# Attention and gated layer on one core: the first head in pieces, probabilities added in pairs on GpSimd, nine key blocks from head 10

## The chip, the cores and the metric

The kernel runs on 1 core of a Trainium2 chip. The metric is the device time of one execution in microseconds; three runs of the kernel before took 936.40, 937.06 and 937.13 us. The engines are named as in the profile: PE is TensorE (matmuls), PEld its weight loads, DVE is VectorE, ACT is ScalarE, POOL is GpSimd, SP is SyncE, which issues DMAs.

## The reference

Attention over q and k of 4 batches × 8 heads × 1152 positions × 64, the query positions averaged in twos, and then a gated layer on the concatenated heads:

```python
q_pool = q.reshape(B, H, S // 2, 2, D).mean(axis=3)
scores = scale * np.matmul(q_pool, k.transpose(0, 1, 3, 2))
scores = scores - np.max(scores, axis=-1, keepdims=True)
attn = np.exp(scores); attn = attn / (np.sum(attn, -1, keepdims=True) + 1e-09)
x = (attn @ v).transpose(0, 2, 1, 3).reshape(B * S // 2, H * D)
out = (1 / (1 + np.exp(-(x @ w_gate))) * (x @ w_val)) @ w_out
```

So there are 32 heads of 576 queries and 1152 keys, and a layer 512 -> 1536 -> 512 over 2304 rows.

## The kernel before, in words

Heads are taken one after the other, in pairs (0 and 1, 2 and 3, ...), eight to a batch. Each head has two halves of 288 queries (`GR`), and each half nine blocks of 128 keys. For a block, two matmuls make the scores in a PSUM bank (line 472: the operands are split in a high and a low part, and the second matmul also carries the maximum of each query, subtracted by a diagonal matrix). ACT makes the exponential (line 476, tile `eh`), in heads 8 and later a second time in full precision (line 504), DVE makes the difference `el` (line 507), and PE multiplies both with V (lines 514 and 518). In heads 0 to 7 (`WHOLE`) one matmul in full float32 does it (line 489, tiles `e` and `ve`).

The sums of the probabilities, from head 8 on, come in two ways. Of the blocks in `POOLC(u)` (seven of nine in heads 8 to 13, nine of nine from head 14) POOL adds the `eh` tiles one by one into `acc` (line 536). A block outside it costs one more matmul, of `eh` with ones (line 521). At the end of a half ACT makes the high part of `acc` (line 576, tile `dh`), DVE the low part (line 579), and two matmuls with ones (line 583) put the sum into the bank of the low products.

Before a head's scores its operands are made (`head_operands`): q and K are loaded by SP (lines 303 and 300), POOL adds the two query positions (line 316), ACT makes the high parts (lines 321 and 336), DVE or POOL the low parts (lines 326 and 342). Then the maxima: twelve matmuls of 128 queries × 384 keys (line 375), each reduced by DVE (line 380), and the four query tiles' maxima joined (line 390) and written as diagonals into the low operand (line 358, on DVE for head 0, on POOL after it). The last 64 queries of the two heads of a pair share three more matmuls: SP copies their operands together (lines 404 and 405, `KP` and `QP`), and POOL writes their diagonals (line 413).

The gated layer of a batch (`gated`, line 699 for its matmuls, line 756 its low parts on POOL) is interleaved with the heads of the next batch, and the last batch's layer stands alone at the end. The weights are converted during heads 0 to 7 and read back from memory.

The order on each engine is written out by a planner (`Plan`): every operation has an engine, an estimated duration, a priority, the operations it comes after and the buffers it takes (`SLOTS` says how many of each there are). The planner plays the work through with these durations and takes on each engine the ready operation of the lowest priority number; the sequence that comes out is the order on the engine's queue. On the chip each queue runs in that order, and an operation waits where it stands. PE's eight PSUM banks (`b`), eight `eh`, four `el`, two `acc` and two `dh` are the buffers that the halves share.

Of the kernel before, what the change touches and what calls it, by code (L numbers as in the profile page):

```python
# [9 lines left out]
F32 = mybir.dt.float32  # L10
# [12 lines left out]
class Op:  # L23
    def __init__(self, eng, dur, fn, prio, after=(), take=None, late=0.0, keep=0.0):
# [3 lines left out]
        self.users, self.start, self.end = [], None, None  # L28
# [9 lines left out]
class Plan:  # L38
# [16 lines left out]
    def op(self, eng, dur, fn, prio, after=(), uses=(), take=(), late=0.0, keep=0.0):  # L55
        o = Op(eng, dur, fn, prio, after, list(take), late, keep)
        for h in uses:
            o.after.append(h.ops[0])
        for h in list(take) + list(uses):
            h.ops.append(o)  # L60
        self.ops.append(o)
        return o

    def run(self):
        n_dep = {}
        ready = {e: [] for e in self.LAT}
        for k, o in enumerate(self.ops):
# [3 lines left out]
            for a in o.after:  # L71
                a.users.append(o)
        free = {t: [(0.0, s) for s in range(n)] for t, n in self.slots.items()}
# [24 lines left out]
        while done < len(self.ops):  # L98
# [7 lines left out]
            while again:  # L106
                again = False
                for e in self.LAT:
# [40 lines left out]
                    for u in o.users:  # L149
                        n_dep[u] -= 1  # L150
                        u.at = max(u.at, o.end if u.eng == e and e != "SP" else av)
# [7 lines left out]
def attention_glu_kernel(ctx: ExitStack, tc: tile.TileContext, qT, kT, vt_in, v, wg, wv, wo, out):  # L159
# [43 lines left out]
    def change_first():  # L203
# [10 lines left out]
    rc = const.tile([128, GN // 32], F32, name="rc")  # L214
    SK_T = lambda n: [const.tile([128, SK], F32R, name=f"{n}{i}") for i in range(SLOTS["K"])]
    SQ_T = lambda n: [const.tile([128, SQ + 64], F32R, name=f"{n}{i}") for i in range(SLOTS["Q"])]
    SHAPE = {"x": [128, 2, SQ], "wg": [128, 2, 2, 4, 128], "el": [128, GN], "acc": [128, GN],
# [12 lines left out]
        "eh": tiles("eh", [128, GN], F32R),  # L230
# [6 lines left out]
        "pm": tiles("pm", [128, 4, 4], F32),  # L237
# [49 lines left out]
    DGP = lambda u: u >= 1  # L287
    RUNS = (2, 5, 8)
    POOLC = lambda u: range(7 if u < 14 else NC)
    LO, HI = slice(0, 64), slice(64, 128)  # L290


    def head_operands(u, need):
        whole = WHOLE(u)
# [56 lines left out]
        am = maxima(need - 21, pm, 4, lambda t: tl(qh)[0][:, t * 128:(t + 1) * 128], lambda: tl(kh)[0],  # L351
                    lambda: tl(pm), max_in, [qh, kh])

        def diag(eng):
            nm = tl(pm)[:, :, 3]
            q2 = tl(qh)[1][LO, 0:512].rearrange("p (a c) -> p a c", c=64)
            for par, p in enumerate((LO, HI)):
                eng.tensor_tensor(  # L358
                    out=q2[:, par:8:2], in0=ident[p, p].unsqueeze(1).to_broadcast([64, 4, 64]),
                    in1=nm[p].unsqueeze(2).to_broadcast([64, 4, 64]), op=ALU.mult)  # L360

        if DGP(u):
            dg = pl.op("POOL", 1.5, lambda: diag(nc.gpsimd), need - 6, after=[am], uses=[pm, qh])
        else:
            dg = pl.op("DVE", 1.3, lambda: diag(nc.vector), need - 6, after=[am], uses=[pm, qh])
        return dict(k=kh, q=qh, v=vr, lv=lv, got=[dg] + max_in + rest, hi_k=hi_k, hi_q=hi_q)

    def maxima(at, pm, nt, lhs, rhs, out, after, uses):
        red = []
        for t in range(nt):  # L370
            for j in range(3):
                m = pl.hold("b")

                def mm(t=t, j=j, m=m):
                    nc.tensor.matmul(out=tl(m)[:, 0:384], lhsT=lhs(t), rhs=rhs()[:, j * 384:(j + 1) * 384],  # L375
                                     start=True, stop=True)

                def rmax(t=t, j=j, m=m):
                    o = out()[:, t, j:j + 1] if nt > 1 else out()[:, j:j + 1]
                    nc.vector.tensor_reduce(out=o, in_=tl(m)[:, 0:384], axis=AXX, op=ALU.max)  # L380
# [6 lines left out]
        def all_max():  # L387
            o = out()
            if nt > 1:
                nc.vector.tensor_reduce(out=o[:, :, 3], in_=o[:, :, 0:3], axis=AXX, op=ALU.max, negate=True)  # L390
            else:
                nc.vector.tensor_reduce(out=o[:, 3:4], in_=o[:, 0:3], axis=AXX, op=ALU.max, negate=True)  # L392
# [486 lines left out]
```

## Time and profile before

| | |
|---|---|
| median of three runs | 937.06 us |
| the profiled execution | 936.75 us |
| its span, first to last instruction | 935.0 us |
| PE busy | 910.1 us (97%) |
| DVE busy | 679.3 us (73%) |
| ACT busy | 658.5 us (70%) |
| POOL busy | 645.6 us (69%) |

The predicted time is that of a run; the rows come from the profiled execution, which is 1.75 us longer than its span. Heads 0 to 7 occupy about 16 to 153 us, heads 8 to 31 the time up to about 810 us (27 us each), and the last batch's gated layer the rest. PE's records overlap, since a matmul is recorded longer than the distance to the next; a duration per matmul is therefore taken from the distance of starts or from the chain.

### The profile page before, as it was taken

The page shows a single profiled execution, that of the slowest core. Times are in us where ns is not written, and L with a number is a line of the kernel's source. Part 1 is how long each engine was busy: PE and PEld are TensorE (multiplying, and loading weights), DVE is VectorE, ACT ScalarE, POOL GpSimd, SP SyncE. Part 2 cuts the span into 40 slices and gives each one's busy share as a digit, 9 for nine tenths or more (in the row PEclk, how much of TensorE's full clock was granted, in tenths as well). Part 3 has the DMA queues.
Part 4 walks back from the last instruction along what each step waited for, and adds up shares of the span by engine and source line. Part 5 has one row for each costly group of instructions (what it writes and reads, how often), then busy time and mean ns, then how long its engine had stood idle before and what let it go on. Part 6 is the DMA issues. An engine that isn't in the chain of part 4 may idle for free.

```text
span 935.0 us, 18634 instructions
## 1 busy us (share of the span) xinstructions
PE 910.1 (97%) x6312; PEld 878.3 (94%) x6312; DVE 679.3 (73%) x1466; ACT 658.5 (70%) x1701; POOL 645.6 (69%) x744
## 2 busy tenths in 40 slices
PE   5999999999999999999999999999999999999998
PEld 4887887999999999999999999999999999999998
DVE  6578678898899898888777988878778885510112
ACT  4888788989998777677877688677778767422211
POOL 6645456788788688788879889888878877521211
PEclk9999999999999999999999999999999999999999
DMA  8898988787868556554445545644554433444432
GB/s 182 211 283 250 263 260 250 240 262 227 277 200 281 169 206 190 149 161 112 144 126 148 175 132 152 179 147 132 154 152 130 142 113 113 158 142 161 178 113 74
DMA packets 57566, 166.87 MB, mean 178 GB/s; under 512 B 17536, under 2 KB 21632, under 8 KB 51328
## 3 DMA queue, kind: packets, MB, share of 16 engines
q1 hardware_dynamic: 57472, 165.70, 58.3%
q8 instruction: 49, 0.80, 0.4%
q14 instruction: 45, 0.37, 0.1%
HBM read 132.12 MB, written 23.59 MB: 167 GB/s over the span
## 4 chain that ended last, share of the span: by engine, by line
PE 86%; DVE 8%; ACT 4%; issue 1%; DMA 1%; POOL 0%; SPq 0%; ACTq 0%; POOLq 0%; DVEq 0%
PE bank L699 45%; PE bank L472 15%; PE bank L375 7%; PE bank L489 7%; PE bank L518 6%; PE bank L514 5%; DVE pm L380 2%; DVE dh L579 2%; PE bank L583 1%; DVE el L507 1%; DVE pp L380 1%; DMA kr<-in_kT_dram 1%; ACT e L476 1%; ACT eh L476 1%; POOL acc L536 0%
## 5 line engine op out<-in xcount | busy, mean ns | idle before, releaser
L699 PE MATMUL bank<-x,wg 128*128 128x288 f32 x2304 | 357.1, 295 | 2.1 <-DVE pp L392 1.2
L699 PEld LDWEIGHTS bank<-x,wg 128*128 128x128 f32 x2304 | 327.3, 188 | 3.8 <-DVE pp L392 1.4
L536 POOL TENSOR_TENSOR acc<-acc,eh 128x288 f32<-128x288 f32 x312 | 258.4, 828 | 52.6 <-ACT eh L476 37.2
L380 DVE TENSOR_REDUCE pm<-bank 128x1 f32<-128x384 f32 x384 | 204.8, 551 | 58.5 <-PE bank L375 54.3
L476 ACT ACTIVATE eh<-bank 128x288 fp32r<-128x288 f32 x432 | 176.7, 409 | 80.0 <-PE bank L472 72.0
L507 DVE TENSOR_TENSOR el<-bank,eh 128x288 fp32r<-128x288 f32 x432 | 192.9, 452 | 54.1 <-ACT bank L504 49.8
L472 PE MATMUL bank<-QA,KA 128*128 128x288 f32 x576 | 177.7, 311 | 2.6 <-ACT e L476 1.3
L504 ACT ACTIVATE bank<-bank 128x288 f32<-128x288 f32 x432 | 176.6, 409 | 0.1
L472 PE MATMUL bank<-QB,KB 128*128 128x288 f32 x576 | 169.2, 297 | 3.0 <-DVE QB L358 3.0
L756 POOL TENSOR_TENSOR g<-sg,g 128x288 fp32r<-128x288 f32 x96 | 79.1, 824 | 107.8 <-ACT g L752 105.8
L375 PE MATMUL bank<-KA,QA 128*128 128x384 f32 x384 | 131.9, 357 | 9.3 <-ACT KA L336 8.3
L699 PE MATMUL bank<-g,wo 128*128 128x288 f32 x864 | 139.1, 296 | 0.0
L514 PE MATMUL bank<-eh,vt 128*128 128x288 f32 x432 | 127.7, 296 | 0.9 <-DVE el L507 0.9
L518 PE MATMUL bank<-el,vt 128*128 128x288 f32 x432 | 127.9, 297 | 0.7 <-DVE el L507 0.7
L699 PEld LDWEIGHTS bank<-g,wo 128*128 128x128 f32 x864 | 125.7, 189 | 0.3 <-DVE pm L380 0.2
L472 PEld LDWEIGHTS bank<-QA,KA 128*128 128x128 f32 x576 | 109.3, 190 | 9.7 <-ACT e L476 2.9
L472 PEld LDWEIGHTS bank<-QB,KB 128*128 128x128 f32 x576 | 109.3, 190 | 4.9 <-issue 3.4
L748 DVE SCALAR_TENSOR_TENSOR sg<-sg,bank 128x288 f32<-128x288 f32 x96 | 43.2, 450 | 79.8 <-PE bank L699 77.9
L375 PEld LDWEIGHTS bank<-KA,QA 128*128 128x128 f32 x384 | 74.1, 194 | 13.4 <-ACT KA L336 8.6
L518 PEld LDWEIGHTS bank<-el,vt 128*128 128x128 f32 x432 | 81.3, 188 | 1.8 <-DVE el L507 1.5
L514 PEld LDWEIGHTS bank<-eh,vt 128*128 128x128 f32 x432 | 81.2, 188 | 1.5 <-DVE el L507 1.2
L742 ACT ACTIVATE sg<-bank 128x288 f32<-128x288 f32 x96 | 39.3, 409 | 56.7 <-PE bank L699 56.1
(67 smaller groups left out, 1254.6 us busy)
## 6 DMA issues: line engine op xcount, KB each, us to landing
wg<-wg_d SPq DMA_DIRECT2D x48, 1024.0 KB, 5.1
kr<-in_kT_dram SPq DMA_DIRECT2D x64, 288.0 KB, 5.3
wo<-wo_d SPq DMA_DIRECT2D x36, 512.0 KB, 3.9
wg_d<-cs SPq DMA_DIRECT2D x24, 512.0 KB, 4.8
qr<-in_qT_dram SPq DMA_DIRECT2D x32, 288.0 KB, 3.9
KP<-KA SPq DMA_DIRECT2D x32, 288.0 KB, 3.5
vr<-in_v_dram SPq DMA_DIRECT2D x24, 288.0 KB, 3.3
cr<-in_wg_dram SPq DMA_DIRECT2D x12, 512.0 KB, 5.7
```

Of the source, the lines that this page charges most:

```text
L375: nc.tensor.matmul(out=tl(m)[:, 0:384], lhsT=lhs(t), rhs=rhs()[:, j * 384:(j + 1) * 384], start=True, stop=True)
L380: nc.vector.tensor_reduce(out=o, in_=tl(m)[:, 0:384], axis=AXX, op=ALU.max)
L472: nc.tensor.matmul(out=tl(m)[:, 0:GN], lhsT=tl(hd["k"])[k][:, ks], rhs=tl(hd["q"])[k][:, a:b], start=(k == 0), stop=(k == 1))
L476: nc.scalar.activation(out=tl(eh), in_=tl(m)[:, 0:GN], func=ACTF.Exp, scale=1.0 / 16.0)
L489: nc.tensor.matmul(out=tl(av[0])[:, 0:GN], lhsT=pair(c, 0), rhs=tl(h), start=(c == 0), stop=(c == NC - 1))
L504: nc.scalar.activation(out=p, in_=p, func=ACTF.Exp, scale=1.0 / 16.0)
L507: nc.vector.tensor_tensor(out=tl(el), in0=tl(m)[:, 0:GN], in1=tl(eh).bitcast(F32), op=ALU.subtract)
L514: nc.tensor.matmul(out=tl(av[0])[:, 0:GN], lhsT=pair(c, w), rhs=tl(eh), start=(c == 0), stop=(c == NC - 1))
L518: nc.tensor.matmul(out=tl(av[1])[:, 0:GN], lhsT=pair(c, 1 - w), rhs=tl(el), start=(c == 0), stop=(c == NC - 1 and not mine_c))
L536: nc.gpsimd.tensor_tensor(out=tl(acc), in0=tl(e0).bitcast(F32) if two else tl(acc), in1=tl(e1).bitcast(F32), op=ALU.add)
L699: nc.tensor.matmul(out=ps[:, 0:GN], lhsT=l, rhs=r, start=(n == 0 and j == 0), stop=(n == 3 and j == 2))
L756: nc.gpsimd.tensor_tensor(out=g[:, 1, a:b], in0=tl(sg), in1=g[:, 0, a:b].bitcast(F32), op=ALU.subtract)
```

## The change

It has three parts and what goes with them.

Head 0 has its own operand code (`first_head`). q is loaded in two pieces of 384 and 192 columns by SP, K in two halves of 576 columns, the first issued from ACT's queue and the second from SP's; V follows. The sum of the two query positions is made on DVE, per piece, and so are the low parts of q. The 64 queries of the last tile are a fifth tile of the head itself, so there are fifteen maxima; the first nine (three query tiles, enough for the first half of 288) have their own joining and diagonals, on DVE, and the other six the same later, needed by the second half alone. Head 1 also gets five tiles and no shared tail. Three set-up operations are changed: a small Exp activation is put ahead of everything on ACT, and two of the three memsets of the K tiles go from DVE to POOL.

```diff
+    def first_head():
+        QS, KS, TS = ((0, 384), (384, SQ)), ((0, SQ), (SQ, SK)), ((0, 1, 2), (3, 4))
+                nc.sync.dma_start(out=tl(qr)[:, :, a:b], in_=qT[0][:, :, a:b])
+                def load_k(a=a, b=b, p=p, eng=nc.sync if k else nc.scalar):
+                    eng.dma_start(out=tl(kr)[p, a:b], in_=kT[0][:, a:b])
+                nc.vector.tensor_tensor(out=r[:, 0, a:b], in0=r[:, 0, a:b], in1=r[:, 1, a:b], op=ALU.add)
...
+                    a = pl.op("PE", pe(384), mm, -21 + 3 * t + j, after=[max_in[k]] + ([ka[0]] if j == 0 else ka),
+            o = pl.op("DVE", 0.1, lambda ts=ts: all_max(tl(pm), ts), -21 + 3 * ts[-1] + 2.5, after=red, uses=[pm])
+            dg.append(pl.op("DVE", 1.0 if len(ts) > 2 else 0.7, lambda ts=ts: diags(nc.vector, tl(pm), tl(qh), ts),
...
+        return dict(..., got=[dg[0], qb] + max_in + ka + kb, dg1=[dg[1]], ...)
...
+        if p == 0:
+            for h in hd:
+                h["got1"] = h.get("dg1", [])
+            return hd
...
+    nc.vector.memset(warm, 0.0)
+    nc.scalar.activation(out=warm, in_=warm, func=ACTF.Exp)
-        nc.vector.memset(TL["K"][k][1][LO].bitcast(F32), 1.0)
+        (nc.gpsimd if k else nc.vector).memset(TL["K"][k][1][LO].bitcast(F32), 1.0)
```

The probabilities lie two key blocks to a tile (`eh`: four tiles of 2 × 288 instead of eight of 288), and POOL adds two blocks with one operation of 576 elements into an `acc` of 2 × 288, of which there is one instead of two. At the last block, the two halves of `acc` are added (`fold`) and then the ninth (or seventh) block. The low part of the sums is made by POOL instead of DVE.

```diff
-        "eh": 8, "acc": 2
+        "eh": 4, "acc": 1
+            if c in mine_c and c % 2 and c > 1:
+                    nc.gpsimd.tensor_tensor(out=tl(acc), in0=tl(old).bitcast(F32), in1=tl(eh).bitcast(F32), op=ALU.add)
+                added = [pl.op("POOL", 1.48, add, pos + 0.5, after=highs + added, uses=[eh, pr[0] if c == 3 else acc],
+                               take=[acc] if c == 3 else [])]
+            elif c in mine_c and c == mine_c[-1]:
+                    nc.gpsimd.tensor_tensor(out=tl(acc)[:, 0], in0=tl(acc)[:, 0], in1=tl(acc)[:, 1], op=ALU.add)
+                    nc.gpsimd.tensor_tensor(out=tl(acc)[:, 0], in0=tl(acc)[:, 0], in1=tl(eh)[:, 0].bitcast(F32), op=ALU.add)
...
-                nc.vector.tensor_tensor(out=tl(dh)[:, 1], in0=tl(acc), in1=tl(dh)[:, 0].bitcast(F32), op=ALU.subtract)
+                nc.gpsimd.tensor_tensor(out=tl(dh)[:, 1], in0=tl(acc)[:, 0], in1=tl(dh)[:, 0].bitcast(F32), op=ALU.subtract)
-            o = pl.op("DVE", 0.72, acc_lo, at, after=[o], uses=[acc, dh])
+            o = pl.op("POOL", 0.85, acc_lo, at, after=[o], uses=[acc, dh])
```

All nine blocks are added by POOL from head 10 on; before, this began with head 14:

```diff
-    POOLC = lambda u: range(7 if u < 14 else NC)
+    POOLC = lambda u: range(7 if u < 10 else NC)
```

The planner learns one thing: an operation may be planned `behind` another without waiting for it (used for the loads of head 0).

## Rows read from the trace of the kernel before

**Rows 1.** The page, busy time of each engine.
```profile
PE 910.1 (97%) x6312; PEld 878.3 (94%) x6312; DVE 679.3 (73%) x1466; ACT 658.5 (70%) x1701; POOL 645.6 (69%) x744
```
**Rows 2.** Timeline of the start: start us, us, engine line op, tiles, count, idle before.
```profile
4.92 1.28 ACT L321 ACT_TABLE_LOAD   x1 [4.92 <-DMA qr<-in_qT_dram]
...
8.41 2.78 POOL L342 TENSOR_TENSOR KB<-kr,KA 64x576 fp32r<-64x576 f32 x2 [2.10 <-ACT KA L336]
...
9.05 5.78 DVE L380 TENSOR_REDUCE pm<-bank 128x1 f32<-128x384 f32 x12 [1.23 <-PE bank L375]
...
15.06 0.85 DVE L358 TENSOR_TENSOR QB<-ident,pm 64x256 fp32r<-64x256 f32 x2
```
**Rows 3.** The chain in order of time: start us, us, what, count.
```profile
1.99 5.52 DMA kr<-in_kT_dram
...
16.06 2.98 PE bank L472 x11
...
30.05 2.91 PE bank L489 x12
...
511.37 0.18 PE bank L375
...
811.20 120.70 PE bank L699 x909
```
**Rows 4.** Windows: stretch, its length, busy us of each engine, clock, DMA.
```profile
core 0: us, PE busy (x) PEld busy (x) DVE busy (x) ACT busy (x) POOL busy (x), PEclk, DMA share, GB/s
...
2.00:7.50 5.50, 0.00 (x0) 0.00 (x0) 3.26 (x11) 1.97 (x2) 2.84 (x5) 1.00 1.06 210
...
22.80:40.00 17.20, 17.20 (x96) 15.25 (x95) 7.80 (x18) 12.91 (x31) 10.24 (x10) 1.00 0.86 228
...
204.30:260.80 56.50, 56.07 (x403) 54.28 (x401) 50.03 (x107) 51.71 (x134) 45.07 (x50) 1.00 0.83 264
260.80:316.30 55.50, 55.50 (x407) 55.02 (x407) 51.45 (x113) 47.54 (x123) 44.75 (x50) 1.00 0.74 230
316.30:756.00 439.70, 434.16 (x3160) 429.90 (x3160) 363.69 (x788) 331.36 (x883) 369.29 (x430) 1.00 0.50 149
538.70:592.60 53.90, 53.81 (x398) 53.54 (x397) 44.05 (x99) 42.24 (x113) 48.73 (x57) 1.00 0.50 147
...
380.00:383.30 3.30, 3.30 (x16) 3.30 (x15) 2.15 (x5) 1.69 (x4) 1.22 (x3) 0.53 0.05 17
```
**Rows 5.** Waits of PE: who waited for whom, us in total, times, longest.
```profile
PE bank L583 <- DVE dh L579: 3.0, 5, 0.9
```
**Rows 6.** Lines by source: count, duration min/median/max in ns, first and last start.
```profile
L579 DVE TENSOR_TENSOR dh<-acc,dh x48: 440/458/2735, 169.6 to 809.0; 128x288 fp32r<-128x288 f32 x48
...
L507 DVE TENSOR_TENSOR el<-bank,eh x432: 417/457/460, 153.9 to 807.9; 128x288 fp32r<-128x288 f32 x144
...
L342 POOL TENSOR_TENSOR KB<-kr,KA x48: 1402/1428/1604, 8.4 to 736.1; 64x576 fp32r<-64x576 f32 x48
```
**Rows 7.** Timelines of DVE, POOL and PE, 373 to 379 us.
```profile
374.32 2.73 DVE L579 TENSOR_TENSOR dh<-acc,dh 128x288 fp32r<-128x288 f32 x1
...
373.78 1.43 POOL L316 TENSOR_TENSOR qr<-qr 64x576 f32<-64x576 f32 x1
375.17 0.80 POOL L536 TENSOR_TENSOR acc<-eh,eh 128x288 f32<-128x288 f32 x1
375.94 0.80 POOL L624 TENSOR_TENSOR x<-y,x 128x288 fp32r<-128x288 f32 x1
...
377.48 0.40 PE L514 MATMUL bank<-eh,vt 128*128 128x288 f32 x1 [0.86 <-DVE el L507]
378.43 0.40 PE L472 MATMUL bank<-QA,KA 128*128 128x288 f32 x1 [0.56 <-DVE y L562]
```
**Rows 8.** Groups of instructions by line and shape: count, busy us, mean ns.
```profile
L536 POOL TENSOR_TENSOR acc<-acc,eh 128x288 f32<-128x288 f32 x312 | 258.4, 828 | 52.6 <-ACT eh L476 37.2 <-PE bank L699 1.2 <-PE bank L375 0.4
...
L521 PE MATMUL bank<-eh,sel 128*128 128x288 f32 x24 | 7.1, 295 | 0.0
```

More of the change, by code (lines that the diff above doesn't have):

```diff
@@ L23, with __init__ @@
 class Op:
-    def __init__(self, eng, dur, fn, prio, after=(), take=None, late=0.0, keep=0.0):
+    def __init__(self, eng, dur, fn, prio, after=(), take=None, late=0.0, keep=0.0, behind=None):
         self.eng, self.dur, self.fn, self.prio = eng, dur, fn, prio
@@ L27, in __init__ @@
         self.take, self.late, self.keep = take, late, keep
-        self.users, self.start, self.end = [], None, None
+        self.users, self.start, self.end, self.behind, self.next = [], None, None, behind, []
 class Hold:
@@ L53, in hold, with op @@
         return h
-    def op(self, eng, dur, fn, prio, after=(), uses=(), take=(), late=0.0, keep=0.0):
-        o = Op(eng, dur, fn, prio, after, list(take), late, keep)
+    def op(self, eng, dur, fn, prio, after=(), uses=(), take=(), late=0.0, keep=0.0, behind=None):
+        o = Op(eng, dur, fn, prio, after, list(take), late, keep, behind)
         for h in uses:
-            o.after.append(h.ops[0])
+            if behind is None:
+                o.after.append(h.ops[0])
         for h in list(take) + list(uses):
@@ L72, in run @@
                 a.users.append(o)
+            if o.behind:
+                n_dep[o] += 1
+                o.behind.next.append(o)
         free = {t: [(0.0, s) for s in range(n)] for t, n in self.slots.items()}
@@ L148, in run @@
                             heapq.heappush(times, h.end)
-                    for u in o.users:
+                    for u in o.users + o.next:
                         n_dep[u] -= 1
-                        u.at = max(u.at, o.end if u.eng == e and e != "SP" else av)
+                        u.at = max(u.at, o.end if u.behind is o or u.eng == e and not o.late and e != "SP" else av)
                         if n_dep[u] == 0:
@@ L293, in head_operands @@
     def head_operands(u, need):
+        if u == 0:
+            return first_head()
         whole = WHOLE(u)
@@ L349, in head_operands @@
         max_in, rest, hi_k, hi_q = [ql] + ka, [qb] + kb, ka, [qa, qb]
-        am = maxima(need - 21, pm, 4, lambda t: tl(qh)[0][:, t * 128:(t + 1) * 128], lambda: tl(kh)[0],
+        nt = 5 if u == 1 else 4
+        am = maxima(need - 21, pm, nt, lambda t: tl(qh)[0][:, t * 128:min(SQ, t * 128 + 128)], lambda: tl(kh)[0],
                     lambda: tl(pm), max_in, [qh, kh])
[L354 to L365, printed above, removed]
+        dg = pl.op("POOL", 1.5 + 0.3 * (nt == 5), lambda: diags(nc.gpsimd, tl(pm), tl(qh), range(nt)), need - 6,
+                   after=[am], uses=[pm, qh])
         return dict(k=kh, q=qh, v=vr, lv=lv, got=[dg] + max_in + rest, hi_k=hi_k, hi_q=hi_q)
@@ L461, in half @@
         acc = pl.hold("acc") if mine_c else None
-        adds, added = [], None
+        added, highs, pr = [], [], []
         wait, deps = [], []
@@ L466, in half, with ev @@
             pos = need + c
-            eh, m = pl.hold("e" if whole else "eh"), pl.hold("b")
+            if whole or c % 2 == 0:
+                eh = pl.hold("e" if whole else "eh")
+            m = pl.hold("b")
+            def ev(eh=eh, c=c):
+                return tl(eh) if whole else tl(eh)[:, c % 2]
             def mm(c=c, m=m):
```

136 lines of the change are left out of this document (103 added, 33 removed), and 2 rows, old and new, of the table SLOTS.

## The prediction

> **What bounds the kernel now.** I read the busy shares first, then the chain of waits, then the stages. PE is busy 910.1 of 935.0 us, the next engine 73% [rows 1]: TensorE sets the time, and a change pays only by taking matmuls away, by closing a stretch in which PE stands still, or by keeping its clock up. The profiled execution took 936.75 us, 1.75 outside the span, and is 0.3 us under the median of the runs (937.06); my sum is made against 936.75.
>
> PE stands still in three places. First the start: nothing before 8.32 us, and from there to 16.06 us only twelve maxima and one score matmul. The timeline and the chain in order of time show why [rows 2, 3]: K lands at 7.51 (1.99 + 5.52), DVE's twelve reductions take 5.78 us from 9.05 on (0.48 each), two diagonal products 0.85 from 15.06, and PE goes on at 16.06. Soon after PE is full (17.20 of 17.20 us [rows 4]), so whatever the start gives arrives at the end: the last 909 matmuls take 120.70 us without a break, 0.1328 each [rows 3].
>
> Second, heads 14 to 29 (316.3 to 756.0 us): PE is busy 434.16 of 439.70 us, 5.5 us idle [rows 4]. PE's waits put 3.0 us on the matmuls of line 583 waiting for DVE's dh, in five waits [rows 5]. That DVE operation (the low half of the sums, line 579) has a median of 458 ns but runs to 2735 ns [rows 6]. The longest is plain in the two timelines: dh starts at 374.32 while POOL runs 1.43, 0.80 and 0.80 us back to back, and ends in POOL's next gap at 377.05; el is late behind it and PE waits 0.86 and 0.56 us [rows 7]. Right after, PE's granted clock is 0.53 over 380.0 to 383.3 us [rows 4], nearly all at 1.2 of its 2.4 GHz, which costs 0.47 × 3.3 = 1.6 us more. So up to 5.5 + 1.6 = 7.1 us hang on late DVE work here, most of it dh's. Third, the tail behind the last matmul, which the change leaves.
>
> **The change part by part.**
>
> *Start, loads and split.* Now q (288 KB), K (576 KB) and the first v (288 KB) are issued one after the other; DMA moves 210 GB/s over 2.0 to 7.5 us [rows 4], 1155 KB, just these three. New: q in two parts and K's second half from SP, K's first half from ACT, v behind them. If q and K come before v, their 864 KB take 864/210 = 4.1 us, to 6.1; with some overlap I take 6.4, 1.1 us less than 7.51. Maxima can start on K's first half; the first scores need nine reductions, not twelve: 3 × 0.48 = 1.4 us. The first diagonal covers 192 of 256 columns: a quarter of 0.85, 0.2. Together 2.7.
>
> Against it: three POOL jobs become DVE jobs with both inputs in SBUF (q's sum, in two pieces) or are done in pieces (low half, diagonals). The trace shows what such a job does while POOL runs: dh above, 458 to 2735 ns. The diagonals of 15.06 fell into a gap of POOL; the first ones now come near 12.4 us, where POOL has low halves of 1.4 us each [rows 2]. I charge half a chance of a mean wait of 0.7 us, for three such jobs half hidden: 0.5. Start: −2.2. The Trainium skill (SBUF — State Buffer, "Who interferes with whom") states it as a rule: a DVE instruction with two SBUF inputs and a GpSimd instruction that reads SBUF hold the shared pair exclusively, and the second waits fully. By that rule a diagonal that meets POOL loses up to a whole operation, so the start would give 1.3 us instead of 2.7 if one does; by the row of 15.06 alone it gives 2.7.
>
> Bounds. ACT now first runs the Exp table load (1.28 us [rows 2]) and a small activation, so its DMA issues come near 2.75 us by my estimate (DVE starts at 0.85, the first activation after the load takes 0.68), against 1.36 for K's now: 1.4 us later at worst. With two diagonals waiting 1.4 us each this makes −1.4 + 1.6 − 2.8, a loss of 2.6. Best: q's first part and K's first half are 480 KB, 2.3 us, landed at 4.3; then q's chain limits, first maximum near 6.0: 2.3 + 1.6 = 3.9 gained. The table load itself lay ahead of K's landing: worth nothing. POOL takes two of DVE's memsets (1.02 each there) into a stretch where it loses q's sum and was idle 2.10 us before its first low half [rows 2]: nothing. SP's DMAs of the pair's tail (KP, QP) fall away for heads 0 and 1, and DVE's two memsets: nothing on the path, since loads of head 1 wait for kr's release by POOL's low halves.
>
> *Is PE filled from 13.3 on?* DVE owes 6 reductions of head 0 and 15 of head 1: 21 × 0.48 = 10.1 us, so head 1 can start near 25 us after POOL's diagonals. PE has till then 36 scores × 0.133, 18 products with V × 0.243 (12 in 2.91 [rows 3]) and 21 maxima × 0.18 [rows 3]: 4.8 + 4.4 + 3.8 = 13.0 us against 11.7. Filled. At first PE runs slow (eleven scores in 2.98 us from 16.06, 0.27 each, against 0.133 at the end [rows 3]: 288 columns at 1.2 GHz are 0.24); I leave that stretch as long as now. Each of heads 0 and 1 has 15 maxima instead of 12 and a shared 3: three more, +0.5.
>
> *Nine blocks from head 10.* In heads 10 to 13 two matmuls per half go (line 521: 24 now, 16 go [rows 8]): 16 × 0.133 = −2.1; bounds 0 and −2.1.
>
> *POOL.* A pair add has 576 elements; such an operation on POOL (line 342) takes 1.43 [rows 6], a 288-element add 0.83 in the mean [rows 8]. Nine blocks: now 8 × 0.83 = 6.6 us a half; new 3 × 1.43 + fold 0.83 + add 0.83 + low half 0.82 = 6.8. Seven blocks now: 6 × 0.83 = 5.0. So heads 14 on: +0.2 a half; heads 10 to 13: +1.8 a half, 7.2 a pair. POOL is busy 45.07 of 56.50 and 44.75 of 55.50 us there [rows 4]: it goes to 52.3/55.4 = 94% and 96%. The fullest pair now is 48.73 of 53.90, 90% [rows 4], with PE at 53.81. I take no loss, since PE has the gated products as filler; the other bound is below. The single acc and the four paired eh buffers: acc is needed again at the next half's fourth block, some 27/18 × 3 = 4.5 us later, and add, high half (0.44) and low half (0.82) are done in about 2.7: nothing, up to the same bound.
>
> *Low half on POOL.* DVE loses 48 operations, and with them the waits for POOL that they show. Behind the low half on POOL stand adds and operand work; the den matmul waits for it as before. Bounds: −7.1, and +11.4 (the slower rival). I take −4.5, nearer to the first, because dh is the operation named in the waits; not all, because an order laid anew leaves new late places.
>
> Sum: 936.75 − 2.2 + 0.5 − 2.1 − 4.5 = 928.4; as a median 928.5.
>
> **Rivals.**
> - *The stalls come back elsewhere:* el or y late behind POOL, no gain from dh. For it: POOL gets fuller; against: no other DVE operation of these heads has such a spread (el 417 to 460 ns [rows 6]). 928.4 + 4.5 = 932.9.
> - *POOL becomes the bound of heads 10 to 13.* If it can't be filled beyond the 90% seen, the pairs take 52.3/0.904 = 57.9 and 52.0/0.904 = 57.5 instead of 55.4 and 54.4: +5.6, 934.0. Against it: gated products fill PE.
> - *The loads win nothing.* K landing as now leaves only the reductions and the diagonal: 1.1 less, with the waits on the lock doubled 1.6 less: 930.0. For it: the same 16 DMA engines at 106% busy share [rows 4]. The Trainium skill (DMA: Bandwidth & Descriptors, "Issuing engines are not separate DMA queues") says DMAs of several issuing engines interleave on the same engines and only the issuing time is saved; by that rule K's second half lands no earlier and this is the case.
> - *Slower: the low half comes late on POOL.* POOL is in order; while ACT makes the high half (0.44), it may start a pair add or operand of 1.43, and the low half, the den matmul and the release of a PSUM bank slip by about 1 us. Now 5 of 48 halves make PE wait, 0.6 us each. If every second half does, 19 more: +11.4, and no gain: 936.75 − 3.8 + 11.4 = 944.3. It decides from 3.8/0.6, six halves more than now. For it: a fuller POOL; against: the plan gives a pair add 1.48 and a low half 0.85 where the rows say 1.43 and 0.83, so POOL runs ahead of its plan, while DVE's 0.72 for dh was too short.
>
> **How the numbers follow.** Forecast 0.50 (its own range 924.5 to 931.5), stalls elsewhere 0.17, POOL bound 0.09, loads 0.10, late low half 0.14. Low end: best start (−1.7) and all stalls gone (−2.6): 924, taken as 923.5. High end: POOL bound and no gain at the start, 928.4 + 5.6 + 2.2 = 936. What can be told from no change is about 0.2%, 1.9 us. Faster: all of the first four, 0.86, less 0.04 for POOL's bound going further, 0.82; no change 0.06, of which 0.02 from the last rival; slower 0.12, its rest.
>
> **What would show it.** Start: the first score block near 13.3 instead of 16.06, with nine reductions ahead of it, K landed near 6.4, no diagonal over 0.5 us. Nine blocks: 8 matmuls of the old line 521 left. Low half: no wait of PE on dh among the longest, PE idle in heads 14 to 29 near 2 us, no stretch at 1.2 GHz there. POOL: under 96% in heads 10 to 13 with PE full. I am wrong if the den matmul waits in more than ten halves, or if PE is idle over 2 us in heads 10 to 13.

## The result and the profile after

The changed kernel takes 923.18 us in the median of four runs (922.86 to 923.48), against 936.79 (936.40 to 937.13) for the kernel before: a ratio of 0.9855 [0.9838, 0.9872], 13.6 us less. The forecast was 928.5 with a range from 923.5. The sign and the engine that bounds are as forecast; the gain is 5.3 us larger, and the time lies 0.3 us below the range.

The page after, the span and the busy shares:

```profile
span 921.4 us, 18477 instructions
PE 904.3 (98%) x6299; PEld 873.9 (95%) x6299; DVE 649.4 (70%) x1428; ACT 659.9 (72%) x1703; POOL 672.3 (73%) x668
```

Against [rows 1], the span fell by 13.6 us, PE's work only by 5.8, and thirteen matmuls of 6312 are gone: most of the gain is time in which PE stood or ran slowly. DVE has 30 us less to do, POOL 27 more.

The start, as the chain in order of time (start us, us, what), to be read against [rows 2, 3]:

```profile
1.47 4.11 DMA qr<-in_qT_dram
...
5.61 0.35 DVE qr L340
...
5.99 0.55 DVE QA L347
...
6.56 1.49 DVE QA L347
...
9.46 3.36 DVE pm L386 x7
...
13.11 0.84 DVE QB L305
13.96 0.37 DVE QB L305
...
14.46 2.98 PE bank L579 x11
```

The chain now begins with q, not with K. Twice a DVE operation with both inputs in SBUF is far too long: q's second low half (192 columns) takes 1.49 us where the first (384 columns) takes 0.55, and the diagonals take 0.84 and 0.37. The timeline of the same stretch (start us, us, engine and line, tiles, shape, count) shows what lay beside them, and K's loads:

```profile
0.74 0.56 ACTq L326 DMA_DIRECT2D kr<-in_kT_dram  x1
1.34 1.28 ACT L953 ACT_TABLE_LOAD   x1 [1.34 <-PEq L985]
5.61 0.67 ACT L358 ACTIVATE KA<-kr 128x576 fp32r<-128x576 f32 x1
6.42 2.89 POOL L361 TENSOR_TENSOR KB<-kr,KA 64x576 fp32r<-64x576 f32 x2 [0.93 <-ACT KA L358]
6.69 5.63 PE L381 MATMUL bank<-KA,QA 128*128 128x384 f32 x15 [6.69 <-DVE QA L347]
6.94 0.68 ACT L358 ACTIVATE KA<-kr 128x576 fp32r<-128x576 f32 x1 [0.41 <-DMA kr<-in_kT_dram]
12.34 1.40 POOL L424 TENSOR_TENSOR qr<-qr 64x576 f32<-64x576 f32 x1
13.11 1.21 DVE L305 TENSOR_TENSOR QB<-ident,pm 64x192 fp32r<-64x192 f32 x2
```

POOL's low half of K runs from 6.42, its sum of head 1's q from 12.34 to 13.74; both DVE operations end soon after a POOL operation does (the diagonal at 13.95 behind 13.74). The first maximum is at 6.69 (8.32 before), the first block of scores at 14.46 (16.06 before).

The windows after, with the columns of [rows 4]: the stretch at half clock, heads 10 and 11, heads 12 and 13, heads 14 to 29:

```profile
14.40:17.80 3.40, 3.34 (x13) 3.28 (x14) 3.33 (x10) 2.45 (x6) 0.00 (x0) 0.53 0.10 32
197.30:251.80 54.50, 54.50 (x396) 53.58 (x395) 47.07 (x103) 51.71 (x135) 48.72 (x49) 1.00 0.88 276
251.80:307.50 55.70, 55.25 (x398) 53.81 (x397) 50.38 (x113) 47.77 (x123) 50.22 (x50) 1.00 0.75 237
307.50:741.50 434.00, 432.91 (x3161) 428.68 (x3160) 341.17 (x755) 333.44 (x885) 383.63 (x371) 1.00 0.51 152
```

In heads 14 to 29 PE is idle for 1.1 us (5.5 before), and the half-clock stretch of [rows 4] at 380 us has gone. POOL is at 89% and 90% in heads 10 to 13. PE's waits (us in total, times, longest) no longer name dh:

```profile
PE bank L381 <- DVE QA L347: 6.7, 1, 6.7
PE bank L579 <- DVE QB L305: 1.7, 1, 1.7
PE bank L579 <- DVE el L615: 1.2, 2, 0.8
PE bank L815 <- DMA wo<-wo_d: 0.9, 1, 0.9
```

dh by its source line, now on POOL (min, median and max in ns), against [rows 6]:

```profile
L695 POOL TENSOR_TENSOR dh<-acc,dh x48: 797/809/1323, 161.7 to 796.2; 128x288 fp32r<-128x288 f32 x48
```

The last matmul ends at 931.9 us before and at 918.2 after, 13.7 us earlier. Where the 13.7 us came from is read by counting 36 score matmuls to a head in both timelines and taking the start of each head's first; each column is one profiled execution:

| stretch | before | after | difference | forecast |
|---|---|---|---|---|
| to head 0's first scores | 16.1 | 14.5 | −1.6 | −2.2 |
| head 0 | 17.5 | 16.4 | −1.1 | +0.5 |
| heads 1 to 9 | 170.7 | 166.4 | −4.3 | 0 |
| heads 10 to 13 | 112.0 | 110.2 | −1.8 | −2.1 |
| heads 14 to 29 | 439.7 | 434.0 | −5.7 | −4.5 |
| heads 30, 31 and the last layer | 175.9 | 176.7 | +0.8 | 0 |

(The forecast's +0.5 also holds head 1's extra maxima.) The row that asks for a reason is the third.

### The profile page after: what moved, and what is told of

Same layout as the page of the kernel before. It is cut to its first block, busy times and chain, and to the rows that moved or that the text cites. A ratio compares the mean times of both kernels' runs of the same rounds, so it can differ in the third digit from the quotient of the medians.

```text
span 921.4 us, 18477 instructions
## 1 busy us (share of the span) xinstructions
PE 904.3 (98%) x6299; PEld 873.9 (95%) x6299; DVE 649.4 (70%) x1428; ACT 659.9 (72%) x1703; POOL 672.3 (73%) x668
## 4 chain that ended last, share of the span: by engine, by line
PE 93%; DVE 3%; ACT 2%; DMA 1%; issue 0%; POOL 0%; SPq 0%; ACTq 0%; DVEq 0%; POOLq 0%
PE bank L815 48%; PE bank L579 16%; PE bank L473 8%; PE bank L597 7%; PE bank L626 6%; PE bank L622 6%; PE bank L699 1%; DMA wo<-wo_d 1%; DMA qr<-in_qT_dram 0%; DVE pm L479 0%; DVE pm L386 0%; DVE el L615 0%; ACT e L583 0%; POOL acc L654 0%; DVE pp L479 0%
## 5 line engine op out<-in xcount | busy, mean ns | idle before, releaser
L479 DVE TENSOR_REDUCE pm<-bank 128x1 f32<-128x384 f32 (+1 forms) x375 | 200.5, 551 | 52.6 <-PE bank L473 49.0
L644 POOL TENSOR_TENSOR acc<-acc,eh 128x576 f32<-128x576 f32 x92 | 132.8, 1444 | 17.3 <-ACT eh L583 15.4
L473 PE MATMUL bank<-KA,QA 128*128 128x384 f32 (+1 forms) x375 | 126.9, 347 | 1.4 <-ACT e L583 0.7
L644 POOL TENSOR_TENSOR acc<-eh,eh 128x576 f32<-128x576 f32 x48 | 68.7, 1431 | 13.9 <-ACT eh L583 9.7
```

The source lines that it names most:

```text
L473: nc.tensor.matmul(out=tl(m)[LO if t == 4 else ALL, 0:384], lhsT=lhs(t), rhs=rhs()[:, j * 384:(j + 1) * 384], start=True, stop=True)
L479: nc.vector.tensor_reduce(out=o, in_=tl(m)[p, 0:384], axis=AXX, op=ALU.max)
L644: nc.gpsimd.tensor_tensor(out=tl(acc), in0=tl(old).bitcast(F32), in1=tl(eh).bitcast(F32), op=ALU.add)
```

## The experiments

Each ratio is to the kernel before on the same chip, with its 95% interval; us are worked out as the ratio's distance from 1 times 936.8. Times by head are each from the one profiled execution of a run.

**The parts alone.** e1_start is the kernel before with the part on the start:

```diff
+    def first_head():
...
+        if u == 0:
+            return first_head()
```

> The start part alone (first head in pieces, five tiles in heads 0 and 1, warm activation, memsets); everything from head 8 on as before. Theory A (the start gives what its own trace shows: first scores at 14.46 instead of 16.06, TensorE's slow stretch ending near 17.8 instead of 21.6 us, and about 2 us of stalls less in heads 1 to 7): 4 to 5 us faster than before, 932 to 933. Rival (the start gives only its 1.6 us, and the rest of the lead at head 8 comes from another order around the low half and the pairs): 1.0 to 2.0 us faster, 935 to 936.

932.28 us, 0.9956 [0.9939, 0.9972]: −4.1. Head 1 starts 2.0 earlier, but head 8 4.1 earlier. The gain doubles between the two, where only head 1's five tiles differ in what is executed; its order is that of the changed kernel up to 150 us on PE, DVE, ACT and POOL.

e2_lowpool is the kernel before with dh's low half on POOL:

```diff
-                nc.vector.tensor_tensor(out=tl(dh)[:, 1], in0=tl(acc), in1=tl(dh)[:, 0].bitcast(F32), op=ALU.subtract)
+                nc.gpsimd.tensor_tensor(out=tl(dh)[:, 1], in0=tl(acc), in1=tl(dh)[:, 0].bitcast(F32), op=ALU.subtract)
-            o = pl.op("DVE", 0.72, acc_lo, at, after=[o], uses=[acc, dh])
+            o = pl.op("POOL", 0.85, acc_lo, at, after=[o], uses=[acc, dh])
```

> The kernel before with only the low half of the sums moved from VectorE to GpSimd. Theory A (the shared port: VectorE's operation with two SBUF inputs stood still while GpSimd worked, and that cost PE's waits in heads 8 to 29): 6 to 9 us faster, 928 to 931, and no wait of PE on dh. Rival (the low half waits as long in GpSimd's queue as it did for the port): within 2 us of before.

929.48 us, 0.9927 [0.9908, 0.9946]: −6.8. Heads 14 to 29 take 433.7 us instead of 439.7, and PE no longer waits for dh: near the upper end (7.1) of what I had put on it.

**Is it the lock, or DVE's load?** In e3_lowpsum the low half stays on DVE but reads one input from PSUM:

```diff
-                nc.vector.tensor_tensor(out=tl(dh)[:, 1], in0=tl(acc), in1=tl(dh)[:, 0].bitcast(F32), op=ALU.subtract)
+                nc.vector.tensor_tensor(out=tl(dh)[:, 1], in0=tl(av[0])[:, 0:GN], in1=tl(dh)[:, 0].bitcast(F32), op=ALU.subtract)
-            o = pl.op("DVE", 0.72, acc_lo, at, after=[o], uses=[acc, dh])
+            o = pl.op("DVE", 0.72, acc_lo, at, after=[o, last], uses=[acc, dh, av[0]])
```

> The kernel before with the low half still on VectorE at the same place, but one of its two inputs read from PSUM (the bank of the high product) instead of SBUF; the low half's values are thus not the sums' low part, the work is the same. Theory A (port): the operation takes 0.46 us at most everywhere instead of up to 2.7, and the time falls by about as much as with the low half on GpSimd, 6 to 9 us. Rival (VectorE has too much to do, so that taking 0.46 us off it per half is what helps): the operation is still there, so no more than 2 us faster.

934.29 us in the median of ten runs (932.96 to 939.20), 0.9986 [0.9972, 1.0]: −1.3, a miss of the time expected. But dh by its source line in e3_lowpsum is never long:

```profile
L579 DVE TENSOR_TENSOR dh<-bank,dh x48: 439/457/459, 175.9 to 812.1; 128x288 fp32r<-128x288 f32 x48
```

and its heads 14 to 29 (window, columns as before) are as short as e2_lowpool's, with as many DVE operations as before (786, and 788 in [rows 4]):

```profile
324.40:758.50 434.10, 432.28 (x3160) 428.23 (x3160) 350.92 (x786) 330.68 (x881) 365.49 (x430) 1.00 0.51 151
```

Nor did these operations only miss POOL's: by the timelines 33 of the 48 start while POOL works, and none is long, where in the kernel before 27 do and 16 take over 0.6 us. So in the stage that the stalls were read from, the two SBUF inputs are the cause, not DVE's share. The time was lost ahead of it: the first diagonals took 2.09 us beside POOL's work, scores began at 17.2, and head 14 began 8.1 us later than in the kernel before. Of that 3.5 stood ahead of head 8, and up to there the order on PE, DVE, ACT and POOL is that of the kernel before, so that part is neither the order nor the PSUM bank, which this form holds for longer; besides the diagonals there is a wait of PE for ACT of 1.9 us at 85.8, with a granted clock of 0.50 behind it (88.7 to 92.1 us). The other 4.6 came in heads 8 to 13. The profiled run was the slowest of the ten (939.20).

**The low half and the start together.** e4_lowdve is the changed kernel with e2_lowpool's two lines turned back:

```diff
-                nc.gpsimd.tensor_tensor(out=tl(dh)[:, 1], in0=tl(acc)[:, 0], in1=tl(dh)[:, 0].bitcast(F32), op=ALU.subtract)
+                nc.vector.tensor_tensor(out=tl(dh)[:, 1], in0=tl(acc)[:, 0], in1=tl(dh)[:, 0].bitcast(F32), op=ALU.subtract)
```

> The changed kernel with only the low half put back on VectorE. Theory A (port): the dh operation again takes up to 2 or 3 us, the longer pair adds make the wait worse, and 6 to 9 us of the gain go: 929 to 932. Rival (the pair adds alone free the queue, so that the low half has gaps): 923 to 925.

931.25 us, 0.9944 [0.9929, 0.9958]: −5.2. The low half is worth 8.3 us in the changed kernel. PE's waits in e4_lowdve name it again (line 699 is here the matmul that takes the sums):

```profile
PE bank L699 <- DVE dh L695: 2.3, 6, 0.7
```

e8_startlow has the start and the low half only (single adds, two `acc`, seven blocks to head 13):

```diff
-        ... "eh": 4, ... "acc": 1, ...
+        ... "eh": 8, ... "acc": 2, ...
-    POOLC = lambda u: range(7 if u < 10 else NC)
+    POOLC = lambda u: range(7 if u < 14 else NC)
...
-                    nc.gpsimd.tensor_tensor(out=tl(acc), in0=tl(old).bitcast(F32), in1=tl(eh).bitcast(F32), op=ALU.add)
+                        nc.gpsimd.tensor_tensor(out=tl(acc), in0=tl(e0).bitcast(F32) if two else tl(acc),
+                                                in1=tl(e1).bitcast(F32), op=ALU.add)
```

> The start part and the low half on GpSimd together; single adds, two acc, seven blocks up to head 13 as before. Theory A (the two parts act in different stages, so they add): 4.1 + 6.8 = 10.9 us faster than before, 925 to 926, and the pairs and the nine blocks are then worth 2 to 3 us. Rival (they overlap, a stall that one removes is the one that the other removes): 8 to 9 us faster, 927 to 928.

923.63 us, 0.9865 [0.9849, 0.9881]: −12.6. Two of the parts make all but 1 us of the gain; the rest, worth 1.0 by the ratios, lies inside the intervals. Up to head 10 its heads start where the changed kernel's do, to 0.1 us; heads 10 to 13 are 3.0 us longer (113.2), and from head 14 to the end it is 2.9 faster.

**Nine blocks.** e5_seven is the changed kernel with seven blocks to head 13:

```diff
-    POOLC = lambda u: range(7 if u < 10 else NC)
+    POOLC = lambda u: range(7 if u < 14 else NC)
```

> The changed kernel with seven of nine blocks up to head 13, as before. Theory A (16 matmuls of 0.133 us are the whole effect): 2.1 us slower than the changed kernel, 925 to 926. Rival (GpSimd at 92 to 95% in heads 10 to 13 takes most of it back): within 0.7 us of the changed kernel.

923.55 us, 0.9863 [0.9847, 0.9880]: −12.8. The nine blocks are worth 0.4 us by the medians and 0.75 by the ratios, and cannot be told from nothing; sixteen matmuls at 0.133 would be 2.1. POOL in heads 10 to 13 falls from 48.72 and 50.22 us to 46.42 and 46.20 (windows 198.6 to 254.0 and 254.0 to 309.9 us). Those heads are 1.1 us longer than in the changed kernel (111.3), and the time behind them is 1.8 shorter: what the blocks and the pairs gain in their own stage later stages give back, by these traces.

This run shows one thing more. Up to 213 us its order on PE, DVE, ACT and POOL is that of the changed kernel, and its heads 1 to 9 take the same 166.4 us; yet head 0 takes 17.6 us instead of 16.4, because the half clock behind the first scores goes on for longer. A window of the changed kernel and the same of e5_seven (columns of [rows 4]):

```profile
17.80:20.20 2.40, 2.40 (x15) 1.96 (x13) 0.39 (x2) 2.35 (x6) 2.07 (x2) 1.00 0.00 0
...
17.80:20.20 2.40, 2.40 (x7) 1.69 (x5) 0.36 (x2) 2.35 (x5) 1.90 (x2) 0.50 0.00 0
```

So the same instructions in the same order can have the shorter or the longer stretch; what decides it, no run shows.

**The order.** e6_nostart is the changed kernel with the old start, that is, the kernel before with the low half, the pairs and the nine blocks:

```diff
-    def first_head():
...
-        if u == 0:
-            return first_head()
```

> The changed kernel with the start as before. Theory A (the start is worth 4.1 us, of which 2 lie ahead of head 1 and 2 in another order of heads 1 to 8): 4 us slower than the changed kernel, 927 to 928, with PE's wait for the last maxima at the border to head 8 back. Rival (the lead at head 8 comes of the order after it as well): 1.5 to 2.5 us slower, 925 to 926.

931.86 us, 0.9953 [0.9936, 0.9970]: −4.4. Taking the start away costs 9.2 us. By the profiled executions 1.7 of it stand ahead of the first scores, 2.4 in head 0, 1.7 in heads 1 to 7 and 3.9 in heads 8 and 9. What differs there is the order at the border from the pair 6, 7 to head 8. In PE's timeline of the kernel before, the maxima of the next pair stand in one row with nothing beside them, and then PE waits for DVE:

```profile
156.30 2.37 PE L375 MATMUL bank<-KA,QA 128*128 128x384 f32 x6
159.82 2.38 PE L699 MATMUL bank<-x,wg 128*128 128x288 f32 x16 [1.15 <-DVE pp L392]
```

After the change they stand one by one between scores and products of head 8, as in these lines of its timeline, and there is no such wait:

```profile
153.12 0.33 PE L579 MATMUL bank<-QA,KA 128*128 128x288 f32 x1
...
153.42 0.40 PE L626 MATMUL bank<-el,vt 128*128 128x288 f32 x1
153.65 0.34 PE L473 MATMUL bank<-KA,QA 128*128 128x384 f32 x1
```

e6_nostart has the row and the wait back (1.1 us). The theory: a start that the plan sees 1 to 2 us earlier lets the planner lay the heads out anew, and the layout is worth about as much as the start. To test it without touching an instruction, e12_late is the changed kernel whose loads of head 0 the planner believes 0.5 us later:

```diff
-            lq.append(pl.op("SP", 0.6, load_q, -60 + 2 * k, uses=[qr] if k else [], take=[] if k else [qr], late=2.4,
+            lq.append(pl.op("SP", 0.6, load_q, -60 + 2 * k, uses=[qr] if k else [], take=[] if k else [qr], late=2.90,
-                                take=[kr] if new else [], late=2.6, behind=lk[-1] if lk else None))
+                                take=[kr] if new else [], late=3.10, behind=lk[-1] if lk else None))
```

> The changed kernel with one pair of planner numbers changed: the first head's loads are planned to land 0.5 us later. No instruction differs; the planner's order of heads 0 to 8 does: the six maxima of heads 8 and 9 stand in one row ahead of the gated layer's first matmul again, as before. Theory B (what the start gives is for a good part the order that comes out of it): 3 to 7 us slower than the changed kernel, 926 to 930, with PE's wait of about 1.1 us at that border back. Rival (the start gives its time by its own instructions): within 1 us of the changed kernel.

929.22 us, 0.9912 [0.9884, 0.9940]: −8.2, so 5.3 of the gain by the ratios (6.0 by the medians) is gone with the same instructions in another order. First scores are at 14.5 as in the changed kernel; head 1 is 1.3 us later than there, head 8 2.0 and head 10 5.9. The 1.3 can't be laid to the order: the half clock behind the first scores lasts as long as in e5_seven (0.50 from 17.8 to 20.2 us). PE's timeline of e12_late at the border is the old one:

```profile
153.48 2.36 PE L473 MATMUL bank<-KA,QA 128*128 128x384 f32 x6
156.99 4.07 PE L815 MATMUL bank<-x,wg 128*128 128x288 f32 x18 [1.15 <-DVE pp L490]
```

and the window behind the wait is at half clock, fifteen matmuls in 3.4 us:

```profile
157.00:160.40 3.40, 3.40 (x15) 3.40 (x16) 3.29 (x8) 1.99 (x5) 2.90 (x5) 0.53 0.81 182
```

The wait belongs to the order; the half clock behind it need not follow. In the kernel before sixteen matmuls take 2.38 us there. In e3_lowpsum, whose order is the same up to that place and beyond, they are slow, as a line of PE's timeline and the window show:

```profile
163.33 4.20 PE L699 MATMUL bank<-x,wg 128*128 128x288 f32 x18 [1.15 <-DVE pp L392]
...
163.80:167.10 3.30, 3.30 (x16) 3.30 (x15) 3.19 (x8) 1.94 (x4) 2.88 (x5) 0.50 1.04 233
```

e13_early turns it round: the kernel before, its loads of head 0 planned 1 us earlier, no instruction different.

```diff
-        lq = pl.op("SP", dma(288), load_q, need - 40, take=[qr], late=3.0)
-        lk = pl.op("SP", dma(576), load_k, need - 40, take=[kr], late=3.0)
+        lq = pl.op("SP", dma(288), load_q, need - 40, take=[qr], late=3.0 if u else 2.0)
+        lk = pl.op("SP", dma(576), load_k, need - 40, take=[kr], late=3.0 if u else 2.0)
```

> The kernel before with the first head's loads planned 1 us earlier; no instruction differs, but the order does, and the maxima of heads 8 and 9 are interleaved with the gated layer's first products. Theory B (order): 2 to 4 us faster than before, 932 to 934, with the first scores at 16 us as before. Rival: within 1 us of before.

934.49 us in the median of ten runs, 0.9967 [0.9951, 0.9982]: −3.1, with the first scores at 16.0 as before and the maxima interleaved at the border. Heads 1 to 7 take 117.4 us instead of 119.0 and heads 8 and 9 49.7 instead of 51.7. e15_lowearly puts the same two lines on e2_lowpool:

> The kernel before with the low half on GpSimd and the first head's loads planned 1 us earlier: the old start, single adds, seven blocks. Theory B: the low half's 6.6 and the order's 2 to 4 us add, 925.5 to 927.5. Rival (order effects don't carry over to another order): 929 to 931, the low half alone.

926.71 us, 0.9884 [0.9854, 0.9914]: −10.9, without any work on the start. The two numbers of the plan add 4.1 by the ratios (2.8 by the medians) to the low half's 6.8; within the intervals, what the order gives and what the low half gives add up.

All fourteen profiled executions together, heads 1 to 9 in us, sorted by the start and by how the maxima stand at the border:

| | maxima interleaved | maxima in a row |
|---|---|---|
| old start | e13_early 167.1, e15_lowearly 168.2 | kernel before 170.7, e2_lowpool 169.9, e3_lowpsum 175.9, e6_nostart 172.0 |
| new start | changed kernel 166.4, e1_start 168.1, e4_lowdve 166.9, e5_seven 166.4, e8_startlow 166.5, e14_portwait 166.7 | e10_port 170.7, e12_late 171.0 |

It is the order and not the start that parts the short from the long.

**What the lock takes at the start.** e10_port tried to hold POOL back in the plan only:

```diff
-            kb.append(pl.op("POOL", pool(SQ), k_lo, -12 + k, after=[o], uses=[kr, kh]))
+            kb.append(pl.op("POOL", pool(SQ), k_lo, -12 + k, after=[o] + max_in, uses=[kr, kh]))
...
-            o = pl.op("ACT", act(SQ), v_hi, need - 4, after=[hd["lv"]], uses=[hd["v"]], take=[stat])
+            o = pl.op("ACT", act(SQ), v_hi, need - 4, after=[hd["lv"]] + (first_dg if u == H else []), uses=[hd["v"]], take=[stat])
```

> The changed kernel with GpSimd kept off the port at the start: its low halves of K come after VectorE's low half of q, and head 8's V split after the first diagonals. Theory A (VectorE's second q operation took 1.49 us and the first diagonal 0.84 because GpSimd held the port, 1.1 and 0.5 us too long, both on the chain to the first scores): first scores near 13 us, 1.0 to 1.6 us faster than the changed kernel, 921.6 to 922.2. Rival (head 1's K comes later for it and PE runs out of work before head 1): within 0.5 us of the changed kernel.

930.76 us, 0.9944 [0.9925, 0.9964]: −5.2, a miss. On the chip POOL's low half reads nothing that DVE writes, so nothing held it, and q's second low half took 1.49 us as before; the first diagonal, now beside two POOL operations back to back, took 2.43 (0.84 in the changed kernel); and the plan fell back into the old order, with a wait of 1.1 us at the border. It does not test what the lock takes at the start, and is one more case of the old order.

e14_portwait makes POOL wait in fact: two copies of one column, each reading what DVE must have written first, ahead of POOL's low halves of K, and of head 1's q sum and head 8's V:

```diff
+        def hold_q():
+            nc.gpsimd.tensor_copy(out=held[HI, 0:1], in_=tl(qh)[0][HI, SQ - 1:SQ].bitcast(F32))
+
+        hq = pl.op("POOL", 0.1, hold_q, -13, after=max_in, uses=[qh])
-            kb.append(pl.op("POOL", pool(SQ), k_lo, -12 + k, after=[o], uses=[kr, kh]))
+            kb.append(pl.op("POOL", pool(SQ), k_lo, -12 + k, after=[o, hq], uses=[kr, kh]))
...
+            nc.gpsimd.tensor_copy(out=held[LO, 1:2], in_=tl(qh)[1][LO, 383:384].bitcast(F32))
+
+        holds.append(pl.op("POOL", 0.1, hold_d, -30, after=[dg[0]] + kb, uses=[qh]))
```

> The changed kernel in which GpSimd really waits at the start: two one-column copies that read VectorE's results stand ahead of its low halves of K, and ahead of head 1's query sum and head 8's V split. (In the run before this one, e10_port, these waits were only in the plan and not in the instructions.) The order around head 8 is that of the changed kernel. Theory A (the port held up VectorE by 1.1 us in q's second low half and 0.5 in the first diagonal): the two operations take 0.35 and 0.64 us, first scores at 12.6 to 13.2 us instead of 14.46, 1.0 to 1.8 us faster than the changed kernel, 921.4 to 922.2. Rival (head 1 comes later for the waits): within 0.5 us.

921.92 us (921.41 to 922.49), 0.9833 [0.9806, 0.9860]: −15.6, the lowest median of the study. Its timeline of the start:

```profile
5.83 0.98 DVE L348 TENSOR_TENSOR QA<-qr,QA 64x384 fp32r<-64x384 f32 x2
6.96 0.18 POOL L356 COPY held<-QA 64x1 f32<-64x1 f32 x1 [1.48 <-DVE QA L348]
7.11 2.79 POOL L366 TENSOR_TENSOR KB<-kr,KA 64x576 fp32r<-64x576 f32 x2
12.48 0.72 DVE L306 TENSOR_TENSOR QB<-ident,pm 64x192 fp32r<-64x192 f32 x2
13.35 0.37 PE L589 MATMUL bank<-QB,KB 128*128 128x288 f32 x1 [1.19 <-DVE QB L306]
```

q's low halves fall from 2.05 us to 0.98, the diagonals from 1.21 to 0.72, and the scores begin 1.1 us earlier. The median is 1.3 us under the changed kernel's; the two intervals overlap, but the rows show the place. Of the 1.1 us, 0.6 is left at head 30; the last matmul ends 1.6 earlier, as the changed kernel's wait of 0.9 us for the last weights is missing here.

## Why the prediction came out as it did

*What bounds it.* Right: PE at 98%, and the gain is idle PE. Three of the four rivals did not come: dh's stalls did not reappear, POOL stayed under its bound, and dh on POOL has a maximum of 1323 ns and no wait of PE that names it. The one on the loads came in part, as the rows on the start show.

*The step that failed* is "whatever the start gives arrives at the end": a pure shift. The forecast gave heads 1 to 9 nothing, in the sum and in the low end of the range, and they became 4.3 us shorter. A kernel whose order comes from a planner is not shifted by an earlier start; the plan is made again, and every later head may stand differently. e12_late and e13_early show it with no instruction changed: 0.5 us in the plan took 5.3 us away, 1 us gave 3.1. One place is shown, the border to head 8, with its wait of 1.15 us. Heads 8 and 9 are 2.2 us shorter after the change, of which the wait is half; in e13_early they are 2.0 shorter. The other 2.1 us, in heads 1 to 7, are spread over gaps that no row of a view names; e13_early has 1.6 of them with no instruction changed, so they too are mostly the order's. Not all that e12_late lost is: in its profiled execution the half clock behind the border costs 0.47 × 3.4 = 1.6 and the longer one at the start 1.3, and both are seen without a change of order (e3_lowpsum, e5_seven).

*The start itself* was forecast at −2.2 and then +0.5 for three maxima, −1.7 by head 1; it gave −1.6 by the first scores and −2.7 by head 1. Ahead of the first scores the sum is near; its parts are not.
- The loads did better than the bound feared: ACT issued K's first half at 0.74, ahead of its table load, not near 2.75. K's two halves were copied from 5.61 and 6.94; before, K landed at 7.51 [rows 3]. K's second half landed near 6.9, between my 6.4 and the 7.51 of the rival on the loads. The Trainium skill (DMA: Bandwidth & Descriptors, "Issuing engines are not separate DMA queues") says that DMAs of several issuers share the same engines and only issuing time is saved. The trace agrees in so far as the whole of q and K was in near 6.9, not 6.1; what made the first maximum 1.6 us earlier was that it needs K's first half and q's first piece alone (q's low part was made at 6.54 instead of 7.81).
- The lock took more than the 0.5 charged: 1.14 on q's second low half (1.49 against 0.35 for the sum of the same 192 columns at 5.61) and 0.47 on the diagonals (0.84 against 0.37), 1.6 together. I had said that a diagonal over 0.5 us would show this step wrong, and it does. e14_portwait gave 1.1 of it back. The Trainium skill (SBUF — State Buffer, "Who interferes with whom") has the rule: a DVE instruction with two SBUF inputs and a reading GpSimd instruction exclude each other, and the later one waits fully. e3_lowpsum, e14_portwait and the start all agree with it, and weighing it as a rule rather than as half a chance would have been nearer at this step.
- The stretch at half clock behind the start was left as long as before. PE's timeline of before shows how long it was: eleven scores about 0.24 apart, and seven maxima in 2.23 us, 0.32 each where 0.18 is the distance elsewhere [rows 3], so that PE was slow until about 21.2 (the granted clock has no record there before 21.3). After the change its granted clock is 0.53 from 14.4 to 17.8, and the scores at 19.0 are 0.13 apart. The seven maxima at half rate cost 7 × (0.32 − 0.18) = 1.0 us by my estimate, about the −1.1 of head 0. That 1.1 is luck: e5_seven, with the same instructions in the same order, has a head 0 of 17.6 us, as long as before (17.5). What PE did ahead of it was fifteen maxima from 6.69 on instead of twelve from 8.32.

```profile
16.06 0.58 PE L472 MATMUL bank<-QB,KB 128*128 128x288 f32 x1 [3.04 <-DVE QB L358]
...
18.84 2.44 PE L375 MATMUL bank<-KA,QA 128*128 128x384 f32 x7
21.07 1.74 PE L489 MATMUL bank<-e,ve 128*128 128x288 f32 x6
```

*Low half on POOL.* Mechanism right, the size too small in the whole. −4.5 was taken from a range that ended at −7.1; heads 14 to 29 alone gave −5.7, the whole −6.8 alone (e2_lowpool) and 8.3 in the changed kernel (e4_lowdve). The reservation, that a new order would bring new late places, was wrong in that stage: PE's idle time went to 1.1 us (2 forecast), and the stretch at 1.2 GHz is gone. That stretch I had laid to the waits, and this is not shown: e1_start, e4_lowdve and e13_early have dh on DVE, up to 2.8, 1.9 and 2.2 us long in heads 14 to 29, and no such stretch, and take 438.9, 438.6 and 437.9 us there. Against these the stage gave 3.9 to 4.9 us, near the 4.5; the rest of what the low half gave lies outside it (heads 10 to 13 take 113.7 us in e4_lowdve, 110.2 in the changed kernel).

*Nine blocks.* Eight matmuls of the old line 521 are left, as forecast, and heads 10 to 13 are 1.8 shorter, but e5_seven puts no more than about 0.75 on the nine blocks in the whole time. POOL's adds were priced rightly, yet POOL came to 89 and 90%, not 94 and 96. POOL's groups of the changed kernel in heads 10 and 11 (line, shape, count, busy us, mean ns) tell why:

```profile
L644 POOL TENSOR_TENSOR acc<-acc,eh 128x576 f32<-128x576 f32 x8 | 11.5, 1441 | 1.8 <-ACT eh L583 1.6
L644 POOL TENSOR_TENSOR acc<-eh,eh 128x576 f32<-128x576 f32 x4 | 5.7, 1428 | 1.0 <-PE bank L815 0.9
L651 POOL TENSOR_TENSOR acc<-acc 128x288 f32<-128x288 f32 x4 | 3.2, 809 | 0.2
L654 POOL TENSOR_TENSOR acc<-acc,eh 128x288 f32<-128x288 f32 x4 | 3.2, 808 | 0.3
L695 POOL TENSOR_TENSOR dh<-acc,dh 128x288 fp32r<-128x288 f32 x4 | 3.2, 807 | 0.2
...
L424 POOL TENSOR_TENSOR qr<-qr 64x576 f32<-64x576 f32 x1 | 1.4, 1420 | 0.0
```

and the same groups of the kernel before, in its heads 10 and 11:

```profile
L536 POOL TENSOR_TENSOR acc<-acc,eh 128x288 f32<-128x288 f32 x20 | 16.2, 810 | 3.5 <-ACT eh L476 2.6
...
L316 POOL TENSOR_TENSOR qr<-qr 64x576 f32<-64x576 f32 x3 | 4.3, 1428 | 0.0
...
L536 POOL TENSOR_TENSOR acc<-eh,eh 128x288 f32<-128x288 f32 x4 | 3.2, 807 | 3.2 <-ACT eh L476 3.1
```

The sums take 26.8 us of POOL instead of 19.4, 7.4 more where I had 7.2. But the planner moved two of q's sums out of the stretch (2.9 us); I had taken all other work there as fixed, which is the same failing as at the start. Pairs, one `acc` and four `eh` buffers cost nothing and gave nothing that can be measured in the whole time (e8_startlow against e5_seven: 0.9865 and 0.9863).

*Together,* the 5.4 us between forecast and result by the stages (5.3 by the medians): +0.6 ahead of the first scores, −1.6 in head 0, −4.3 in heads 1 to 9, +0.3 in heads 10 to 13, −1.2 in heads 14 to 29, and +0.8 at the end, where PE waits once 0.9 us for a load of the last weights.

*Open:* why the pairs and nine blocks without the start (e6_nostart, −4.4) are slower than the low half alone (e2_lowpool, −6.8) beyond a half clock at the border; how e3_lowpsum's 4.6 us in heads 8 to 13 divide between its PSUM bank, its order and the half clock at the border (0.50 over 3.3 us, 1.6); and what decides how long PE stays at half clock.

## What to carry to other kernels

Where a planner writes the order, a change at the start is a new draw of the whole order: price the border between stages beside the shift, give the range several us for it, and try the plan's own numbers (two of them gave 3.1 us here without touching an instruction). A DVE operation whose maximum is several times its median, beside a busy POOL and with both inputs in SBUF, is worth moving or protecting, and here nearly all the idle time behind it in that stage was its price. An order in the plan is no wait on the chip: POOL stayed off while DVE read only where it had data to wait for (e14_portwait, not e10_port). And before a stage is credited to a change, look at the granted clock in it: 1.2 us of head 0 came and went here with nothing changed ahead of it.

## What the runs showed of the hardware that was not expected

- The same wait of 1.1 to 1.15 us of PE, behind the same six maxima, is followed by sixteen matmuls at full rate in the kernel before (2.38 us) and in e2_lowpool, and by 3.3 to 3.4 us at a granted clock of 0.50 to 0.54 in e3_lowpsum, e6_nostart and e12_late. The order does not tell them apart (it is the same in the first two and e3_lowpsum), and nothing else in the rows does.
- The half clock behind the first scores, too, is not fixed by instructions and order: 0.53 over 14.4 to 17.8 us and then 1.00 in the changed kernel, 0.50 still from 17.8 to 20.2 in e5_seven.
- ACT's table load did not delay its first DMA: issued at 0.74 us, the load at 1.34 to 2.62, the second DMA at 1.40 beside it.
- Kernels with the same instructions at the start, on DVE and POOL, can meet the lock or miss it: the first two diagonals took 0.85 us in the kernel before [rows 2] and 2.09 in e3_lowpsum, and 1.21 in the changed kernel and 2.80 in e10_port.
